# The offsets that order the stages of an attention, FNet and feed-forward kernel, set anew

## The chip, the cores and the metric

The kernel runs on one core of a Trainium2 chip. The metric is the device time of one execution in microseconds (us); several executions are timed and their median is taken. The engines are PE (TensorE, matmuls and transposes), DVE (VectorE), ACT (ScalarE), POOL (GpSimd) and SP (SyncE, which here only issues DMAs); PEld is PE's loading of weights. Each engine works off its own instructions strictly in the order in which they were issued, and an instruction that has to wait holds up all that stand behind it on its engine.

## What is computed

Eight batches of 8 heads, 576 positions and 64 channels each are put through two attentions, whose sum x (8 x 576 x 512) goes through a Fourier mix, a normalization and a feed-forward network:

```python
def _attn_ref(q, k, v):
    ...
    q_d = q.reshape(B, H, Sd, factor, D).mean(axis=3)      # factor 4, Sd = 144
    ...
    out_d = sm_attn(q_d, k_d, v_d)
    out_up = np.repeat(out_d, factor, axis=2)
    mask = np.abs(pos[:, None] - pos[None, :]) < factor
    scores = scale * np.matmul(q, k.transpose(0, 1, 3, 2))
    scores = np.where(mask, scores, -1000000000.0)
    ...
    return (out_up + out_local).astype(np.float32)

def _moe_ref(x, w_ch1, w_ch2):
    X = np.fft.fft(x, axis=1)
    X = np.fft.fft(X, axis=2)
    mixed = np.real(X).astype(np.float32)
    u = x + mixed
    ...
    un = (u - mu) / np.sqrt(var + 1e-06)
    ch = np.maximum(un @ w_ch1, 0.0) @ w_ch2
    return (u + ch).astype(np.float32)
```

## The kernel before

**Pooled attention** (class `Pooled`, one for each batch, called P0 to P7 here). Four copies of v are added up in `vsum`, the first by a DMA from SP, the other three by accumulating DMAs that POOL issues (`sum_v`, L245 to 251). DVE adds up q and k by fours (`sum_in`, L379, five sums for each batch, one for each unit). Then come four steps, each for two heads: scores `sp` on PE (L262), maxima on DVE (L267), exponentials on ACT (L278), transposes `tp` (L288), copies on ACT (L299), the product `avd` with `vsum` (L307) and the division into `odt` (L318 to 322). The result is stored to `ud` in DRAM from SP (L331 to 336).

**Local attention** (class `Unit`, five for each batch, U0.0 to U7.4 here). A unit loads `qkT` (L361, six buffers) and `vaug` (L365, three buffers) from SP; scores `sc` (L386, L393), maxima (L406), exponentials (L411), transposes `tpl` (L423), copies (L443 to 445), products `av` (L452) and the division into `xa` or `xb` (L466 to 470).

**The Fourier mix** (class `Mix`, M0 to M7). Half sums on DVE (L516) and half differences on POOL (L520) of `xa` and `xb` go to `xs` and `xm`; the channels are folded by DVE into `xeo` (L531, L535, also from `odt`), and split into a high and a low part by ACT (`fh`, L542) and POOL (`fl`, L547). The middle channel goes to `z` on ACT and POOL (L556, L557). Four groups of 15 matmuls `y` (L569, called sequence 0 to 3 here) are followed by a copy on ACT (L575) and a difference on DVE (L578); `yz` (L585) does the same for z. Six groups `mix` (L607, three slots, each even and odd) are added on DVE by `mixed` (L611), POOL unfolds them into `oa` and `xm` (L621), and SP stores them to `um` in DRAM in ten DMAs (`store`, L634 and L635).

**The feed-forward part** works on nine blocks of four tiles. Each tile is loaded from `um` by SP (L706), to which POOL accumulates `ud` (L704); DVE and POOL take its statistics (L713 to 717; `rstd` on POOL), DVE normalizes (`un`, L724), PE transposes (`tpn`, L732), ACT and DVE split the result into `unT` (L738, L741). Then come 16 chunks of weights: `hps` (L761) and `acc` (L779 to 781). The first chunks of block 0 and then of block 1 are worked off while the other weights still come in. The weights are decoded once from 64-bit words, in 64 quarters: fetched into `raw` from SP (L146), sized on ACT (L156), clamped on POOL (L161), joined on DVE (L169 to 175), split on ACT and POOL (L186, L190). Most of the quarters come behind the attention.

**What sets the order.** Every step of all these is entered in one list with a time; the times are sums of a stage's start (20 for each batch, 4 for each unit) and an offset from the table `AT` (L22 to 52). The list is sorted by the time (L904 to 906) and issued in that order:

```python
    with tc.manual_schedule():
        for _, _n, fn in sorted(events, key=lambda e: e[:2]):
            fn()
```

So the offsets are no times on the chip: they only set which step stands ahead of which in each engine's row. Waits between engines follow from the tiles that steps share, and from the buffers that they are given in that order. PSUM banks are given out in turn (`bank`): eight in turn before the feed-forward part, four afterwards.

Four times that closes of memory hang on are worked out from the table too (`t_b`, `t_a`, `t_e`, `t_d`): `close_b` (L830) opens the tiles of block 0 in memory that P7 used, `close_a` (L835) the rest of what the first weights need once the last unit is done.

Of the kernel before, what the change touches and what calls it, by code (L numbers as in the profile page):

```python
# [13 lines left out]
ALU = mybir.AluOpType  # L14
# [6 lines left out]
PACE = 20  # L21
AT = {  # L22

    "pooled": (0.6, -0.5, -1.8, -3.1, -3.53),
    "mix": (18.44, 18, 18),

    "local_steps": (0, 1.49, 2.84, 5.24, 5.74, 7.85, 9.25),
    "pooled_steps": (0, 1.58, 2.63, 5.13, 5.73, 7.82, 9.41),

    "qk": (-11.61, 2.5),  # L30
    "sums": (-3.57, 0.79),
    "sum_v": (-10.83, -9.1, -1.92, 1.96),
    "load_v": (3.13,),

    "store_pooled": (1,),
    "pooled_splits": (0.3, 0.9, 0.26, 1.1, 1.34),

    "halves": (0.26, 3.82, 0.35, 3.58),
    "splits": (1.11, 4, 0.49, 1.7, 2.25),
    "z": (0.86, 9.92, 12.49, 12.91, 14.07),  # L40
    "sequence": (13.12, 1.11, 2.15, 3.28),
    "mixed": (19.5, 1.61, 1.13, 2.66, 2.85),

    "ffn": (7.51, 1.51),

    "decode": (49.7, 10.23, 5.84, 1.23, 2.64),
    "decode_steps": (-0.57, 0.24, 0.83, 1.83, 2.17),
    "first_norms": (0.83, 0.7, 2.16, 0.81),
    "second_norms": (-0.5, 0.43, 0.64, 0.83),

    "add": (2.5, 2.04, 2.98),
}


# [11 lines left out]
def kernel(  # L66
# [68 lines left out]
    class Quarter:  # L135


        def __init__(self, n):
            self.f, self.w, self.j = n // 4, 1 + n // 2 % 2, n % 2
            self.n = n  # L140
# [73 lines left out]
    def bank(name, rows=P):  # L214
        banks.append(banks.pop(0))
        return banks[-1].tile([P, DM], F32, name=name, tag="ps")[:rows]
# [21 lines left out]
    sums = {}  # L238
# [253 lines left out]
    halves = [[pf.tile([P, NSL, DM + 2], F32, name=f"x{h}{i}") for h in "sm"] for i in range(2)]  # L492
# [13 lines left out]
    class Mix:  # L506


        def __init__(self, b):
            self.b, self.x, self.y = b, {}, {}  # L510
            self.fh = self.z = None


# [79 lines left out]
        def mix(self, t, odd):  # L593

            n = slots[t][1]
            cols = slice(P * t, P * t + n)
            ps = self.ps = bank("mix", n)
            mms = []
            for T in (2 * odd, 2 * odd + 1):
                mh, ml = chanm[:, 0, T, :], chanm[:, 1, T, :]  # L600
                lh, ll = self.yh[:, T, cols], self.yl[:, T, cols]
                mms += [(lh, mh), (lh, ml), (ll, mh)]
            if not odd:
                mms.append((yz[:, cols], signs.unsqueeze(1).to_broadcast([P, HD, 2])))
            for i, (l, r) in enumerate(mms):
                to = ps if len(r.shape) == 2 else ps.rearrange("p (n two) -> p n two", two=2)
                nc.tensor.matmul(to, l, r, start=(i == 0), stop=(i == len(mms) - 1))  # L607

        def mixed(self, t, odd):
            x = (self.xm if odd else self.xs)[: slots[t][1], t, :DM]  # L610
            nc.vector.scalar_tensor_tensor(  # L611
                out=x, in0=x, scalar=0.5, in1=self.ps, op0=ALU.mult, op1=ALU.add
            )

        def unfold(self, t):
# [21 lines left out]
        def plan(self):  # L637
# [23 lines left out]
            for T in range(4):  # L661
                u = t + first + step * T
                at(u, self.sequence, T)
                at(u + high, self.sequence_high, T)
                at(u + low, self.sequence_low, T)
            first, step, mixed, unfold, store = AT["mixed"]
            for i in range(NSL):
                for odd in range(2):
                    u = t + first + step * (2 * i + odd)
                    at(u, self.mix, i, odd)  # L670
                    at(u + mixed, self.mixed, i, odd)
                at(u + unfold, self.unfold, i)
# [197 lines left out]
    t = t_a + AT["ffn"][0]  # L870
    starts = {}
    for n, f0, f1 in [(0, 0, ROUND), (1, 0, ROUND), (0, ROUND, NF)] + [(n, ROUND * (n == 1), NF) for n in range(1, NBLK)]:
        starts[n] = t
        t = blocks[n].plan(t, f0, f1)
# [15 lines left out]
    t = 0.0  # L890
    for n, x in enumerate(quarters):
        if x.f < CHUNKS[0]:
            decode(n, first + step * n, ahead)
        else:
            begin = [t_a + ahead_later, t_e, t_d][sum(x.f >= c for c in CHUNKS[1:3])]
            t = max(t + step_later, begin + 0.3)
# [139 lines left out]
```

## Time and profile before

| what | us |
|---|---|
| median of 3 executions | 1250.11 |
| lowest and highest of them | 1248.47, 1251.0 |
| the profiled execution, its own time | 1254.06 |
| its span (first to last instruction) | 1252.0 |
| from the first `hps` to the end of the span | 821.32 |

The profiled execution is 3.95 us longer than the median. Its span leaves out 2.06 us of its own time. The span has two parts. Up to 430.68 us the attentions and the mix of eight batches run interleaved: the pooled attention and the units of one batch beside the mixes of the two batches ahead of it. From there on, PE works off the blocks of the feed-forward part with hardly a gap. A stretch of a batch begins, in the rows below, where PE takes up the first `sp` of that batch: batch 1 at 48.60 us, batch 2 at 93.22 us. The granted clock of PE, 1.00 being 2.4 GHz, is a mean over a stretch; 0.50 is the lower level, 1.2 GHz.

### The profile page before, as it was taken

The page shows a single profiled execution, that of the slowest core. Times are in us where ns is not written, and L with a number is a line of the kernel's source. Part 1 is how long each engine was busy: PE and PEld are TensorE (multiplying, and loading weights), DVE is VectorE, ACT ScalarE, POOL GpSimd, SP SyncE. Part 2 cuts the span into 40 slices and gives each one's busy share as a digit, 9 for nine tenths or more (in the row PEclk, how much of TensorE's full clock was granted, in tenths as well). Part 3 has the DMA queues.
Part 4 walks back from the last instruction along what each step waited for, and adds up shares of the span by engine and source line. Part 5 has one row for each costly group of instructions (what it writes and reads, how often), then busy time and mean ns, then how long its engine had stood idle before and what let it go on. Part 6 is the DMA issues. An engine that isn't in the chain of part 4 may idle for free.

```text
span 1252.0 us, 20525 instructions
## 1 busy us (share of the span) xinstructions
PE 1184.1 (95%) x8336; PEld 981.2 (78%) x8336; DVE 590.7 (47%) x1218; ACT 356.0 (28%) x1038; POOL 318.2 (25%) x397
## 2 busy tenths in 40 slices
PE   5889998899995699999999999999999999999998
PEld 5777887787984578888888888888888888888887
DVE  3767778698877788853222222122122222221211
ACT  3655454555562333431111111111011111111100
POOL 2226355365456566531010010000100100100000
PEclk7888998999997799999999999999999999999999
DMA  9755484565645525314040120210400400300000
GB/s 293 197 169 134 128 238 110 162 196 172 163 127 153 133 77 155 119 51 101 5 97 1 52 50 1 78 25 1 99 3 1 101 1 1 101 1 1 34 1 34
DMA packets 50462, 111.45 MB, mean 89 GB/s; under 512 B 6120, under 2 KB 6248, under 8 KB 50040
## 3 DMA queue, kind: packets, MB, share of 16 engines
q1 hardware_dynamic: 42000, 88.66, 22.6%
q0 software_dynamic: 8368, 21.48, 9.3%
q8 instruction: 66, 1.08, 0.4%
q14 instruction: 28, 0.23, 0.1%
HBM read 81.82 MB, written 28.34 MB: 88 GB/s over the span
## 4 chain that ended last, share of the span: by engine, by line
PE 81%; DVE 10%; DMA 6%; POOL 1%; SPq 1%; issue 1%; ACT 1%; POOLq 0%
PE hps L761 31%; PE acc L779 10%; PE acc L781 10%; PE acc L780 10%; PE y L569 4%; PE mix L607 4%; DMA vsum<-in_vg_dram 3%; PE av L452 2%; DMA qkT<-in_qk_dram 2%; PE avd L307 2%; PE sc L393 1%; DVE sums L379 1%; DVE xeo L535 1%; PE tpn L732 1%; PE sp L262 1%
## 5 line engine op out<-in xcount | busy, mean ns | idle before, releaser
L761 PE MATMUL hps<-unT,w1h 128*128 128x512 f32 x1152 | 311.5, 392 | 0.6 <-DVE yl L578 0.6
L769 DVE SCALAR_TENSOR_TENSOR hl<-hps,hh 128x512 fp32r<-128x512 f32 x144 | 99.3, 690 | 437.3 <-ACT hh L765 437.3
L761 PEld LDWEIGHTS hps<-unT,w1h 128*128 128x128 f32 x1152 | 215.2, 188 | 46.7 <-DVE yl L578 0.8
L765 ACT ACTIVATE hh<-hps 128x512 fp32r<-128x512 f32 x144 | 86.2, 598 | 512.1 <-PE hps L761 512.0
L779 PE MATMUL acc<-w2h,hh 128*128 128x512 f32 x576 | 226.5, 393 | 0.0
L781 PE MATMUL acc<-w2h,hl 128*128 128x512 f32 x576 | 225.1, 391 | 0.0
L780 PE MATMUL acc<-w2l,hh 128*128 128x512 f32 x576 | 225.0, 391 | 0.0
L761 PE MATMUL hps<-unT,w1l 128*128 128x512 f32 x576 | 155.2, 391 | 0.0
L761 PEld LDWEIGHTS hps<-unT,w1l 128*128 128x128 f32 x576 | 108.1, 188 | 23.8
L781 PEld LDWEIGHTS acc<-w2h,hl 128*128 128x128 f32 x576 | 108.2, 188 | 23.6
L779 PEld LDWEIGHTS acc<-w2h,hh 128*128 128x128 f32 x576 | 108.1, 188 | 22.9
L780 PEld LDWEIGHTS acc<-w2l,hh 128*128 128x128 f32 x576 | 108.2, 188 | 22.8
L717 POOL TENSOR_TENSOR rstd<-rstd,mhalf 128x1 f32<-128x1 f32 x36 | 20.3, 564 | 341.4 <-DVE rstd L716 341.4
L704 POOL DMA_DIRECT2D ut<-ud x40 | 35.5, 1111 | 208.0 <-DMA ut<-um 207.7
L607 PE MATMUL mix<-chanm,yh 128*128 128x512 f32 (+1 forms) x192 | 65.8, 425 | 5.6 <-DVE xs L611 3.7
L411 ACT ACTIVATE sb<-sc,mx 128x64 f32<-128x64 f32 x320 | 69.8, 329 | 1.3
L741 DVE TENSOR_TENSOR unT<-tpn,unT 128x512 fp32r<-128x512 f32 x36 | 24.8, 690 | 90.4 <-ACT unT L738 90.4
L547 POOL TENSOR_TENSOR fl<-xeo,fh 128x512 fp32r<-128x512 f32 (+1 forms) x40 | 56.0, 1404 | 30.5 <-ACT fh L542 30.2
L379 DVE TENSOR_REDUCE sums<-qkT 128x224 f32<-128x896 f32 (+4 forms) x48 | 44.5, 947 | 27.9 <-DMA qkT<-in_qk_dram 19.6
L520 POOL TENSOR_TENSOR xm<-xa,xb 128x512 f32<-128x512 f32 x24 | 34.2, 1427 | 87.9 <-DVE xb L470 79.9
L738 ACT CAST unT<-tpn 128x512 fp32r<-128x512 f32 x36 | 21.0, 586 | 113.5 <-PE tpn L732 113.5
L452 PE MATMUL av<-vaug,pT 64*64 64x65 f32 x1280 | 48.5, 227 | 1.7 <-DVE odt L322 1.5
(102 smaller groups left out, 1579.7 us busy)
## 6 DMA issues: line engine op xcount, KB each, us to landing
qkT<-in_qk_dram SPq DMA_DIRECT2D x40, 512.0 KB
raw<-in_wq_dram SPq DMA_DIRECT2D x64, 256.0 KB
vaug<-in_vw_dram SPq DMA_DIRECT2D x40, 260.0 KB
ud<-odt SPq DMA_DIRECT2D x16, 576.0 KB
out_dram<-ut SPq DMA_DIRECT2D x36, 256.0 KB
ut<-um SPq DMA_DIRECT2D x32, 256.0 KB
ut<-ud POOLq DMA_DIRECT2D x32, 256.0 KB, 5.6
vsum<-in_vg_dram POOLq DMA_DIRECT2D x24, 292.5 KB, 4.5
```

The costliest lines, as they stand in the source:

```text
L379: nc.vector.tensor_reduce(out=to, in_=x[:, :, a - g0 : e - g0], axis=AX.X, op=ALU.add)
L411: nc.scalar.activation(out=self.sb[:, a], in_=self.sc[:, a * W : (a + 1) * W], func=AF.Exp, scale=0.125, bias=self.mx[:, a : a + 1],)
L452: nc.tensor.matmul(av[r, a, :], pT[r, 4 * hh + a], va[r, 4 * hh + a, :], start=True, stop=True)
L547: nc.gpsimd.tensor_sub(out=l, in0=self.x[t], in1=h.bitcast(F32))
L569: nc.tensor.matmul(y, l, r, start=(i == 0), stop=(i == len(mms) - 1))
L607: nc.tensor.matmul(to, l, r, start=(i == 0), stop=(i == len(mms) - 1))
L761: nc.tensor.matmul(hps, a[:, c, :], unT[:, x, c, :], start=(i == 0), stop=(i == len(mms) - 1))
L765: nc.scalar.activation(out=hh, in_=self.hps[f], func=AF.Relu)
L769: nc.vector.scalar_tensor_tensor(out=hl, in0=self.hps[f], scalar=0.0, in1=self.hh[f].bitcast(F32), op0=ALU.max, op1=ALU.subtract)
L779: nc.tensor.matmul(acc, hh, w2h, start=start, stop=False)
L780: nc.tensor.matmul(acc, hh, w2l, start=False, stop=False)
L781: nc.tensor.matmul(acc, hl, w2h, start=False, stop=stop)
```

## The change

All offsets of `AT` are set anew, each by less than 6 units of its list time. No operation is added, removed or given another shape. Since several `mix` results of one batch may now be open at a time, `Mix.ps` becomes a dictionary with an entry for each slot and half. Two lines of the table stand for the rest:

```diff
-    "sum_v": (-10.83, -9.1, -1.92, 1.96),
+    "sum_v": (-12.68, -6.88, -1.99, 2.95),
...
-    "mixed": (19.5, 1.61, 1.13, 2.66, 2.85),
+    "mixed": (21.24, 1.83, 2.15, 4.71, 7.35),
...
-            self.b, self.x, self.y = b, {}, {}
+            self.b, self.x, self.y, self.ps = b, {}, {}, {}
...
-            ps = self.ps = bank("mix", n)
+            ps = self.ps[t, odd] = bank("mix", n)
...
-                out=x, in0=x, scalar=0.5, in1=self.ps, op0=ALU.mult, op1=ALU.add
+                out=x, in0=x, scalar=0.5, in1=self.ps[t, odd], op0=ALU.mult, op1=ALU.add
```

What this does to the rows of the engines is shown at three places.

**Place A: SP, the loads of batch 4's units.** `um_66` is the DRAM result of M1, `qkT` and `vaug` are inputs of units of batch 4. Before, the last three of the ten stores, behind which a part of the loads stands:

```order
L634 DMA um_66<-xm_136 56x2x512
L634 DMA um_66<-xm_136 2x1x512
L635 DMA um_66<-xm_136 3x512
L361 DMA qkT<-in_qk_dram 128x1024
L365 DMA vaug<-in_vw_dram 128x520
L361 DMA qkT<-in_qk_dram 128x1024
L146 DMA raw<-in_wq_dram 128x512
L361 DMA qkT<-in_qk_dram 128x1024
L365 DMA vaug<-in_vw_dram 128x520 x2
```

After, the loads, behind which the first of the ten stores stands:

```order
L361 DMA qkT<-in_qk_dram 128x1024
L365 DMA vaug<-in_vw_dram 128x520
L361 DMA qkT<-in_qk_dram 128x1024 x2
L365 DMA vaug<-in_vw_dram 128x520
L361 DMA qkT<-in_qk_dram 128x1024
L146 DMA raw<-in_wq_dram 128x512
L365 DMA vaug<-in_vw_dram 128x520
L634 DMA um_66<-oa 56x3x512
```

Before, three of the five `qkT` loads of a batch stand behind the store of the mix; now all five stand ahead of it. The same holds for the other batches that have such a store.

**Place B: POOL, the small `z` of M1** (`xs_135` and `xm_136` are its halves; `oa` and `xm_134` are the unfolding of M0). Before:

```order
L520 TENSOR_TENSOR xm_136<-xa,xb 128x512
L547 TENSOR_TENSOR fl<-xeo,fh 72x512 x2
L251 DMA vsum<-in_vg_dram 72x1040
L557 TENSOR_TENSOR z<-xs_135,z 128x3
L621 TENSOR_TENSOR oa<-xs_133,xm_134 128x512
L621 TENSOR_TENSOR xm_134<-xs_133,xm_134 128x512
```

After:

```order
L520 TENSOR_TENSOR xm_136<-xa,xb 128x512
L547 TENSOR_TENSOR fl<-xeo,fh 128x512
L547 TENSOR_TENSOR fl<-xeo,fh 72x512
L557 TENSOR_TENSOR z<-xs_135,z 128x3
L161 TENSOR_SCALAR wt<-wt 128x256
L251 DMA vsum<-in_vg_dram 72x1040
L621 TENSOR_TENSOR oa<-xs_133,xm_134 128x512
```

The accumulating DMA of `vsum`, which can't be issued before the one ahead of it has landed, stood right ahead of `z`; now it stands behind it.

**Place C: the passage to the feed-forward part, on POOL** (`ut` are the four tiles of block 0, `ud_57` the pooled result of batch 0). Before:

```order
L547 TENSOR_TENSOR fl<-xeo,fh 72x512 x2
L190 TENSOR_TENSOR w2l_87<-wt,w2h_86 128x256
L621 TENSOR_TENSOR oa<-xs_133,xm_134 128x512
L621 TENSOR_TENSOR xm_134<-xs_133,xm_134 128x512
L704 DMA ut_5791<-ud_57 128x512
L704 DMA ut_5792<-ud_57 128x512
L704 DMA ut_5793<-ud_57 128x512
L704 DMA ut_5794<-ud_57 128x512
L547 TENSOR_TENSOR fl<-xeo,fh 128x512
L520 TENSOR_TENSOR xm_136<-xa,xb 128x512
L717 TENSOR_TENSOR rstd<-rstd,mhalf 128x1 x2
L557 TENSOR_TENSOR z<-xs_135,z 128x3
```

After:

```order
L704 DMA ut_5776<-ud_57 128x512
L704 DMA ut_5777<-ud_57 128x512
L704 DMA ut_5778<-ud_57 128x512
L704 DMA ut_5779<-ud_57 128x512
L547 TENSOR_TENSOR fl<-xeo,fh 72x512
L621 TENSOR_TENSOR oa<-xs_133,xm_134 128x512
L621 TENSOR_TENSOR xm_134<-xs_133,xm_134 128x512
L520 TENSOR_TENSOR xm_136<-xa,xb 128x512
L547 TENSOR_TENSOR fl<-xeo,fh 128x512
L557 TENSOR_TENSOR z<-xs_135,z 128x3
L717 TENSOR_TENSOR rstd<-rstd,mhalf 128x1 x2
```

The four loads now stand ahead of two unfoldings and a split that were ahead of them, and six operations stand between them and the first two `rstd`, where two stood.

**The same passage on PE.** `tpn` are the transposes of block 0 (four for each tile), `yz` the matmuls of M7, `mix` the last one of M6. Before:

```order
L607 MATMUL mix<-chanm,yl 64x512
L732 MATMUL tpn<-ident,un 128x128 x8
L585 MATMUL yz<-seqg,z 2x320 x2
L585 MATMUL yz<-seqm,z 2x320 x3
L585 MATMUL yz<-seqg,z 2x320 x2
L585 MATMUL yz<-seqm,z 2x320 x3
L732 MATMUL tpn<-ident,un 128x128 x4
```

After:

```order
L607 MATMUL mix<-chanm,yl 64x512
L585 MATMUL yz<-seqg,z 2x320 x2
L585 MATMUL yz<-seqm,z 2x320 x3
L585 MATMUL yz<-seqg,z 2x320 x2
L585 MATMUL yz<-seqm,z 2x320 x3
L732 MATMUL tpn<-ident,un 128x128 x16
L569 MATMUL y<-seqg,fh 128x320 x2
```

`yz` moved ahead of all `tpn`. Further ahead, two `mix` groups of M6 stood between the last `av` of the kernel and the first `tpn`; now there are four, and sequence 3 and the first two `mix` groups of M6, which stood ahead of the last `avd` (P7's fourth step), stand behind it. On SP the store of M6 moved back past six `raw` fetches.

## Rows read from the trace of the kernel before

**Rows 1.** Windows by stretch: length, busy us (instructions) of PE, PEld, DVE, ACT, POOL; PEclk, DMA share, GB/s

```profile
48.60:93.22 44.62, 40.98 (x556) 35.37 (x556) 29.82 (x75) 25.13 (x89) 14.55 (x17) 0.88 0.54 150
93.22:143.10 49.88, 45.76 (x576) 38.67 (x577) 36.61 (x85) 24.61 (x88) 21.60 (x23) 0.90 0.57 158
189.19:241.87 52.68, 46.91 (x591) 38.89 (x587) 40.13 (x90) 26.95 (x95) 23.94 (x26) 0.94 0.57 154
241.87:288.88 47.01, 44.68 (x587) 37.98 (x587) 40.08 (x93) 26.61 (x95) 24.08 (x26) 0.96 0.62 173
288.88:334.49 45.61, 43.38 (x591) 36.86 (x588) 40.69 (x90) 26.64 (x95) 24.83 (x26) 1.00 0.62 179
391.90:430.68 38.78, 14.71 (x72) 12.04 (x72) 24.68 (x53) 8.64 (x21) 25.80 (x32) 0.65 0.78 193
430.68:1252.00 821.32, 816.54 (x3640) 670.18 (x3638) 270.76 (x497) 137.85 (x272) 114.20 (x164) 1.00 0.17 46
```

**Rows 2.** Timeline before batch 4 (start, length, engine line operation [idle before <-releaser])

```profile
171.29 3.10 SPq L634 DMA_DIRECT2D um<-oa  x4
...
180.51 0.42 SPq L361 DMA_DIRECT2D qkT<-in_qk_dram  x1
...
187.84 1.05 DVE L379 TENSOR_REDUCE sums<-qkT 128x216 f32<-128x864 f32 x1 [0.46 <-DMA qkT<-in_qk_dram]
...
191.43 0.41 PE L288 MATMUL tp<-ident,sd 72*72 72x72 f32 x4 [1.15 <-DVE xb L470]
```

**Rows 3.** Timeline of POOL and PE at the local `z` of batch 1

```profile
117.69 0.84 POOL L251 DMA_DIRECT2D vsum<-in_vg_dram  x1 [3.76 <-DMA vsum<-in_vg_dram]
...
118.80 0.96 PE L585 MATMUL yz<-seqm,z 128*2 128x320 f32 x3 [1.49 <-POOL z L557]
```

**Rows 4.** Window of PE alone: length, busy us (instructions), PEclk, DMA share, GB/s

```profile
115.00:130.00 15.00, 12.58 (x117) 0.66 0.74 177
```

**Rows 5.** The chain that ended last, two of its links on PE

```profile
361.69 2.24 PE y L569 x15
...
379.07 3.02 PE mix L607 x13
```

**Rows 6.** Timeline of the passage to the feed-forward part, all engines

```profile
381.93 1.20 PE L307 MATMUL avd<-vsum,ptd 72*72 72x65 f32 x16
...
390.07 1.39 DVE L172 SCALAR_TENSOR_TENSOR wt<-raw,wt 128x256 int32<-128x256 int32 x1
...
392.03 1.76 SPq L706 DMA_DIRECT2D ut<-um  x4
...
396.82 3.59 POOL L704 DMA_DIRECT2D ut<-ud  x4
...
405.01 0.69 DVE L713 BATCH_NORM_STATS2 st<-ut 128x6 f32<-128x512 f32 x1 [6.99 <-DMA ut<-ud]
...
408.39 1.09 PE L732 MATMUL tpn<-ident,un 128*128 128x128 f32 x4 [16.31 <-DVE un L724]
...
422.44 0.43 ACT L156 ACTIVATE wt<-raw 128x256 f32<-128x256 f32 x1 [7.07 <-DMA raw<-in_wq_dram]
...
424.43 0.90 PE L569 MATMUL y<-seqg,fh 72*128 72x320 f32 x2 [5.40 <-DVE unT L741]
...
430.68 1.10 PE L761 MATMUL hps<-unT,w1h 128*128 128x512 f32 x4
```

**Rows 7.** Groups by line, shapes together: busy us, mean ns | idle before

```profile
L547 POOL TENSOR_TENSOR fl<-xeo,fh 128x512 fp32r<-128x512 f32 (+1 forms) x40 | 56.0, 1404 | 30.5 <-ACT fh L542 30.2
L379 DVE TENSOR_REDUCE sums<-qkT 128x224 f32<-128x896 f32 (+4 forms) x48 | 44.5, 947 | 27.9 <-DMA qkT<-in_qk_dram 19.6
```

**Rows 8.** Groups by line, each shape apart: busy us, mean ns | idle before

```profile
L172 DVE SCALAR_TENSOR_TENSOR wt<-raw,wt 128x256 int32<-128x256 int32 x64 | 43.0, 672 | 2.2
...
L406 DVE TENSOR_REDUCE mx<-sc 128x8 f32<-128x512 f32 x40 | 27.3, 684 | 2.8 <-PE sc L393 2.6
```

**Rows 9.** Timeline of PE: the first scores of batch 1

```profile
48.60 1.24 PE L262 MATMUL sp<-sums 64*72 64x144 f32 x8 [5.36 <-DVE sums L379]
```

More of the change, by code (lines that the diff above doesn't have):

```diff
@@ L22 @@
 AT = {
[L24 to L31, printed above, removed]
-    "sum_v": (-10.83, -9.1, -1.92, 1.96),
[L33 to L41, printed above, removed]
-    "mixed": (19.5, 1.61, 1.13, 2.66, 2.85),
[L44 to L51, printed above, removed]
+    "pooled": (-0.82, -1.16, -2.92, -3.66, -3.97),
+    "mix": (19.33, 19.44, 19.47),
+    "local_steps": (0, 2.01, 2.74, 4.55, 6.44, 7.99, 9.17),
+    "pooled_steps": (0, 1.64, 3.1, 4.52, 5.5, 6.86, 9.7),
+    "qk": (-9.97, 2.23),
+    "sums": (-2.11, 0.4),
+    "sum_v": (-12.68, -6.88, -1.99, 2.95),
+    "load_v": (4.86,),
+    "store_pooled": (1.6,),
+    "pooled_splits": (0.63, 1.63, 0.39, 1.17, 2.21),
+    "halves": (-1.52, 4.16, 1.15, 3.59),
+    "splits": (1.09, 4.71, 0.22, 0.85, 2.73),
+    "z": (1.77, 8.73, 11.56, 12.33, 13.17),
+    "sequence": (15.17, 1.12, 1.12, 2.9),
+    "mixed": (21.24, 1.83, 2.15, 4.71, 7.35),
+    "ffn": (9.61, 1.41),
+    "decode": (49.18, 9.54, 2.02, 1.18, 3.21),
+    "decode_steps": (-0.73, -0.25, 0.7, 1.96, 3.89),
+    "first_norms": (1.46, 0.91, 3.69, 0.74),
+    "second_norms": (-2.92, 1.41, 5.09, 1.68),
+    "add": (1.13, 1.19, 5.36),
 }
```

## The prediction, made before the changed kernel had run

> **What bounds the kernel now.** I read the windows by stretch first, then the timelines at those stretches that are longer than their like, and last the two orders against each other.
>
> From the first `hps` on PE is busy 816.54 of 821.32 us at a granted clock of 1.00 [rows 1]. No operation changes, so this part can't become shorter by more than its 4.8 us of gaps, and I see nothing in the new order that touches it. What can be won lies in the first 430.68 us.
>
> There PE's work is nearly the same for each batch from the third on, so the best stretch shows what a batch needs: 45.61 us, at a clock of 1.00 [rows 1]. The stretch of batch 4 takes 52.68 us, that of batch 5 47.01 us, that of batch 2 49.88 us. In each of these the clock is under 1.00, and PE stands for a part of them. The passage from 391.90 to 430.68 us holds 14.71 us of PE's work in 38.78 us. So PE is the bound, but it loses time in three ways: it waits, it works behind a wait at a lower clock, and at the passage it has nothing to do.
>
> **The passage (place C).** Between the last `avd` of P7 at 381.93 us and the first `hps` at 430.68 us lie 48.75 us [rows 6]. The chain there: SP issues the `um` loads at 392.03 us, POOL the `ud` loads from 396.82 us on, behind two splits, a weight part and two unfoldings; they have landed at 405.01 us, when DVE's statistics begin after 6.99 us of waiting; `tpn` follows at 408.39 us, PE having stood for 16.31 us. Later PE stands 5.40 us ahead of sequence 0 at 424.43 us, because ACT waited 7.07 us for `raw` at 422.44 us, whose fetch stands on SP behind the ten stores of M6 [rows 6].
>
> The new order changes three things. First, sequence 3 and the first two `mix` of M6 stand behind P7's last `avd`: 2.24 us and about 3.02 us [rows 5], 5.3 us of PE's work that now fills a part of the 16.31 us and lies no longer ahead of 381.93 us. Second, M6's store is moved behind six fetches, so the 5.40 us should go. The price is that the six fetches are in front of the store; nobody waits for `um` of M6 until blocks far behind. Third, POOL issues the `ud` loads earlier in its row, but six operations stand then ahead of the first `rstd`, where two stood. Five of these I price at 1.4 us by the mean of L547 [rows 7], the `z` at little: 7 us. If POOL is done with issuing at 400.4 us as before (396.82 + 3.59), it comes to `rstd` at about 407.5 us, beside 406.2 us before, which I take from 405.01 plus the three steps of statistics. So `tpn` comes 1.5 us later against the last `avd`, at 28.0 us behind it instead of 26.5.
>
> From the first `tpn` to the first `hps` it took 22.3 us, and without the 5.40 us it takes 16.9. That makes 28.0 + 16.9 = 44.9 us instead of 48.75, a gain of 3.9 us, and the 5.3 us of work that lie behind 381.93 us now, and ahead of it before, come to it: **-9 us**. Bounds: 0, if the first `tpn` comes later by as much as is won, and -16, if it comes 1.5 us no later and the `ud` loads land earlier by the two splits and two unfoldings that they no longer stand behind (4 by 1.4, 5.6 us). I take 9 because the `um` loads wait for `ud` of P7 to be stored and can't move much against 381.93 us.
>
> **The loads of the next batch (place A).** Before, SP works off the ten stores from 171.29 us on, and can't begin before the mix is unfolded; the last `qkT` load of batch 4 is issued at 180.51 us and its sum begins at 187.84 us, 7.33 us later [rows 2]. PE then waits for what DVE had put off behind the sums: 1.15 us at 191.43 us [rows 2], and more small ones, and works at a lower clock. What it costs is what the stretches have over 45.61 us: 7.07 us for batch 4, 1.40 us for batch 5 [rows 1]. Now all five loads stand ahead of the stores, and need only a free buffer. **-8.5 us**, if both come down to 45.61; bounds -14 (batch 1 and batch 7's part as well, whose stretches begin and end with other work) and 0 (SP's wait goes, but the loads then wait for their buffers).
>
> **`z` ahead of the `vsum` load (place B).** POOL stood 3.76 us with the accumulating load, `yz` on PE stood 1.49 us for `z` behind it [rows 3], and in the 15 us from 115.00 on the granted clock was 0.66 on the mean [rows 4], which is about two thirds of them at 1.2 GHz. The stretch of batch 2 has 4.27 us over 45.61 [rows 1]; I take **-4 us** of it. Bounds -6 and 0. The `vsum` load now waits with fewer instructions behind it that anyone needs soon.
>
> **The start.** In the new order P1's first `sp` stands behind the second `sc` group of batch 0 and the first `av`, which wait for P0's `avd`. The first `sp` of batch 1, now at 48.60 us after a wait of 5.36 us [rows 9], comes then at 50.8 by my laying of the row, with 0.6 us more work done ahead of it: **+2 us**. Bounds 0 and +5, the wait that is there now.
>
> **New short covers.** In the steady part nothing is turned around, but some steps follow each other more closely. Sequence 2 takes the bank of a unit's result, and the `tp` of the first pooled step comes right behind sequence 3. About one sequence group, 2.24 us [rows 5], covers what DVE or ACT have to do meanwhile, which needs about as much. Where such a cover was missing, PE waited 1.15 us [rows 2]. Seven batches by 0 to 1.15 us are 0 to 8 us; I take 0.4 us each, since cover and need are nearly equal: **+3 us**.
>
> **The sum.** -9 - 8.5 - 4 + 2 + 3 = -16.5 us on the profiled execution's 1254.06 us, so 1237.6 us. The median of the runs lies 3.95 us below that execution: 1233.6, so 1234 us. A measurement of this kernel tells changes of about 0.2%, 2.5 us, from none.
>
> **Rival A: POOL becomes the bound of the passage.** The six operations ahead of `rstd` meet DVE's joins, halves and foldings. In the passage of before, a join beside two splits of POOL took 1.39 us at 390.07 us [rows 6], and 0.672 us on the mean of all 64 [rows 8]: 0.7 us lost on one instruction. Nine such meetings on the chain to `tpn` are 6.5 us, with the later issue of the loads that follows 9 us, which is all that the passage wins. Then it is -7.5 us in all, 1246.6 us for the execution and 1242.6 us for the median. For it speaks that POOL is busy 25.80 of 38.78 us there already [rows 1]; against it, that half of these operations lie between the loads' issue and their landing, when DVE has nothing to do. The Trainium skill has a rule for this ("SBUF — State Buffer", section "Who interferes with whom"): an instruction of DVE with two inputs from SBUF and one of GpSimd that reads SBUF hold a shared port pair in turn, each for its whole length. By that rule each meeting costs as much as the POOL operation has left, so the collisions would be nearer to rival A's than to mine; the 1.39 us agree with it.
>
> **Rival B: the sums of a batch come late; slower.** The five sums of a batch, 44.5/8 = 5.6 us [rows 7], now stand in one row on DVE between the results of a batch's second and third unit, with a local maxima of 0.68 us [rows 8] and two results, for which I take three times as much, 2.0 us: 8.3 us. A unit's share of a stretch is 45.61/5 = 9.1 us. Likewise the last `qkT` load can't begin before the fourth unit's scores leave their buffer, and needs 7.33 + 1.05 = 8.4 us [rows 2] where the next batch's `sp` comes a unit's share later, 9.1 us. So both have a margin of 0.7 to 0.8 us. If a load takes over 8.1 us, or DVE is behind by over 0.8 us, PE waits at the third unit's bank or at `sp`, the clock falls, and the stretch is as long as batch 4's was: 7.07 us lost. With three of the six stretches so, it is -16.5 + 21 = +4.5 us: 1258.6 us, 1254.6 us for the median. For it speaks how thin the margin is, and a DMA share of 0.62 in a good stretch [rows 1]; against it, that a load waits for no store any more, and that all margins are above zero.
>
> **Rival C: the waits only move.** PE waits less at one place and as much at the next: the passage gives 4, the loads give 4, the start takes 5, the covers 3: 0 us, 1254 us and 1250 us for the median.
>
> **Chances.** Forecast 0.62 (its own range 1222 to 1242 us), rival A 0.17, rival B 0.13, rival C 0.08. The range goes from 1217 us, which the bounds of the passage and the loads together would go past only by a little, to 1253 us: it takes in A and C, and leaves out most of B and the lower tail. Faster by over 0.2%: the forecast and A nearly whole, 0.79. Within it: C and an edge of A, 0.07. Slower: B and the upper edge of C, 0.14.
>
> **What would show it.** In the changed kernel's windows the stretches of batches 4 and 5 should be near 45.6 us at a clock of 1.00, that of batch 2 near 46. The wait of `yz` for `z` should be gone. From P7's last `avd` to the first `hps` it should be 45 us, with a wait ahead of the first `tpn` of about 12 us and none over 1 us ahead of sequence 0. Batch 1's `sp` should come at 50 to 51 us. The first `hps` should come at about 414 us. I am wrong if PE waits for `sums` or for the bank of sequence 2 in each batch, or if `tpn` comes over 30 us behind that `avd`.

## The result, and the profile after

The changed kernel takes 1232.12 us in the median (1227.79 to 1232.71), the kernel before in the same comparison 1250.55 us: a ratio of 0.9843 (95% interval 0.9812 to 0.9874). Run once more beside later kernels it took 1230.67 us, 0.9829 (0.9803 to 0.9856). The forecast was 1234 us, and faster.

The profiled execution of the changed kernel took 1231.77 us (span 1229.7 us), 22.3 us less than that of before. Where they went is read from windows of PE between the same four places in both kernels: the first `sp` of batch 1, the first `sp` of batch 7, the last `avd`, the first `hps`. First the kernel before, PE alone (length, busy us (instructions), PEclk, DMA share, GB/s); its last stretch stands in [rows 1]:

```profile
48.60:334.49 285.89, 265.61 (x3479) 0.94 0.59 164
334.49:381.93 47.44, 47.30 (x616) 1.00 0.34 97
381.93:430.68 48.75, 24.68 (x182) 0.72 0.70 178
```

The same view of the changed kernel, which has the last stretch too:

```profile
50.79:307.47 256.68, 248.64 (x3450) 0.99 0.63 183
307.47:360.60 53.13, 48.85 (x611) 0.94 0.34 95
360.60:409.01 48.41, 31.26 (x211) 0.75 0.65 166
409.01:1229.70 820.69, 816.29 (x3640) 1.00 0.17 46
```

| from, to | before | after | difference |
|---|---|---|---|
| start to first `sp` of batch 1 | 48.60 | 50.79 | +2.2 |
| to first `sp` of batch 7 | 285.89 | 256.68 | -29.2 |
| to the last `avd` | 47.44 | 53.13 | +5.7 |
| to the first `hps` | 48.75 | 48.41 | -0.3 |
| to the end | 821.32 | 820.69 | -0.6 |

The counts in brackets say what work was moved across the borders. Batches 1 to 6 hold 29 matmuls fewer, the passage 29 more. At 2.24/15 = 0.15 us each [rows 5] that is 4.4 us, the forecast's 5.3 us to within a microsecond. So, between these two executions, batches 1 to 6 won about 25 us, and the passage about 5, since it does more in the same time. Batch 7 up to its last `avd` lost 6 to 7 us. The feed-forward part is as it was.

A part of the passage's 5 us is chance. Five further executions below keep one of the two orders there: with that of before it took 45.53 and 46.27 us (the first two experiments), with the new one 48.64, 46.75 and 48.46 us (the changed kernel again, and the two edits of it that lie elsewhere and move `vsum` and a join). By the means, 46.9 us before and 48.1 after, the passage with its 4.4 us of added work won about 3 us.

The 25 us of batches 1 to 6 are of two kinds. PE's idle time, length minus busy, fell from 20.3 to 8.0 us: 25 waits of 0.2 to 1.9 us, at 18 kinds of steps, became nine of 0.2 to 2.1 us. The rest, some 12 us, is work that no longer ran at the lower clock: 0.94 on the mean before, 0.99 after. Three stretches of the changed kernel, which answer to the rows of batches 2, 4 and 5 in [rows 1]:

```profile
87.96:130.12 42.16, 40.47 (x569) 1.00 0.58 172
...
174.84:218.60 43.76, 42.85 (x592) 1.00 0.66 190
218.60:262.22 43.62, 43.29 (x591) 1.00 0.64 188
```

Batch 5 has 0.3 us of idle time in 43.6, at a clock of 1.00: by PE's idle time another order of the same operations could win no more than that there.

The passage in the changed kernel, first PE (start, length, instruction [idle before <-releaser]):

```profile
386.80 0.96 PE L585 MATMUL yz<-seqm,z 128*2 128x320 f32 x3 [10.46 <-POOL z L557]
...
389.92 1.11 PE L732 MATMUL tpn<-ident,un 128*128 128x128 f32 x4 [0.82 <-DVE un L724]
393.36 1.09 PE L732 MATMUL tpn<-ident,un 128*128 128x128 f32 x4 [2.33 <-DVE un L724]
...
399.11 1.12 PE L732 MATMUL tpn<-ident,un 128*128 128x128 f32 x4 [3.32 <-DVE un L724]
...
409.01 1.09 PE L761 MATMUL hps<-unT,w1h 128*128 128x512 f32 x4
```

These answer to [rows 6]. The wait of 16.31 us is now one of 10.46, ahead of `yz`; the wait ahead of sequence 0 is gone. New are 6 us of waits between the four tiles, since joins of weights (L169 to L175) stand ahead of the second and the fourth `un` on DVE:

```profile
391.39 0.29 DVE L169 TENSOR_SCALAR wt<-wt 128x256 int32<-128x256 int32 x1
...
392.52 0.69 DVE L724 TENSOR_SCALAR un<-ut,mv,rstd 128x512 f32<-128x512 f32 x1
...
394.54 0.48 DVE L169 TENSOR_SCALAR wt<-wt 128x256 int32<-128x256 int32 x1
...
395.51 1.37 DVE L175 SCALAR_TENSOR_TENSOR wt<-raw,wt 128x256 int32<-128x256 int32 x1
...
397.41 1.64 DVE L724 TENSOR_SCALAR un<-ut,mv,rstd 128x512 f32<-128x512 f32 x1
```

The last `un` also takes 1.64 us, beside an unfolding on POOL; where POOL stands still it takes 0.54. Before, a join stood ahead of the third `un` (412.57 to 414.92 us), but there PE had `yz` to work on and waited only 0.52 us. That the joins are the cause is read from these rows; no run took them away. DVE and POOL at the first statistics:

```profile
382.58 0.69 DVE L713 BATCH_NORM_STATS2 st<-ut 128x6 f32<-128x512 f32 x1 [6.46 <-DMA ut<-ud]
383.52 0.15 DVE L716 TENSOR_SCALAR rstd<-mv 128x1 f32<-128x1 f32 x1
```

```profile
380.51 1.91 POOL L621 TENSOR_TENSOR oa<-xs,xm 128x512 f32<-128x512 f32 x1
382.50 1.26 POOL L621 TENSOR_TENSOR xm<-xs,xm 128x512 f32<-128x512 f32 x1
383.72 1.47 POOL L520 TENSOR_TENSOR xm<-xa,xb 128x512 f32<-128x512 f32 x1
385.16 1.25 POOL L547 TENSOR_TENSOR fl<-xeo,fh 128x512 fp32r<-128x512 f32 x1
386.38 0.37 POOL L557 TENSOR_TENSOR z<-xs,z 128x3 fp32r<-128x3 f32 x1
386.72 0.57 POOL L717 TENSOR_TENSOR rstd<-rstd,mhalf 128x1 f32<-128x1 f32 x1
```

The first statistics are done on DVE at 383.67 us, but POOL comes to the first `rstd` at 386.72, 3 us later, working without a gap.

Batch 7 has one wait that the kernel before does not have there. DVE, POOL and PE:

```profile
326.29 2.73 DVE L172 SCALAR_TENSOR_TENSOR wt<-raw,wt 128x256 int32<-128x256 int32 x1
329.06 1.37 DVE L175 SCALAR_TENSOR_TENSOR wt<-raw,wt 128x256 int32<-128x256 int32 x1
330.35 1.48 DVE L535 TENSOR_TENSOR xeo<-xm 128x256 f32<-128x256 f32 x1
...
332.14 0.42 DVE L322 TENSOR_TENSOR odt<-avd,rsd 72x256 f32<-72x256 f32 x1
```

```profile
326.24 1.28 POOL L547 TENSOR_TENSOR fl<-xeo,fh 72x512 fp32r<-72x512 f32 x1 [1.41 <-ACT fh L542]
327.48 1.26 POOL L621 TENSOR_TENSOR oa<-xs,xm 128x512 f32<-128x512 f32 x1
328.82 1.33 POOL L621 TENSOR_TENSOR xm<-xs,xm 128x512 f32<-128x512 f32 x1
330.11 1.44 POOL L520 TENSOR_TENSOR xm<-xa,xb 128x512 f32<-128x512 f32 x1
```

```profile
332.62 0.73 PE L607 MATMUL mix<-chanm,yh 128*128 128x512 f32 x2 [3.58 <-DVE odt L322]
```

L172, L175 and L535, which take 0.42 us where POOL stands still, end 0.28 us after an operation of POOL each time: 329.02 after 328.74, 330.43 after 330.15, 331.83 after 331.55. Three instructions lose 4.3 us, the pooled result behind them is late, and PE stands 3.58 us for the bank that it frees. This is the rule that the prediction cited for its rival A (the Trainium skill, "SBUF — State Buffer", section "Who interferes with whom"): the trace agrees, with whole operations of POOL waited out and not a share of them.

### The profile page after: what moved, and what is told of

The parts are those of the page before. It is cut to its first block, busy times and chain, and to the rows that moved or that the text cites. A ratio compares the mean times of both kernels' runs of the same rounds, so it can differ in the third digit from the quotient of the medians.

```text
span 1229.7 us, 20578 instructions
## 1 busy us (share of the span) xinstructions
PE 1173.7 (95%) x8336; PEld 977.8 (80%) x8336; DVE 595.5 (48%) x1218; ACT 355.8 (29%) x1038; POOL 312.1 (25%) x397
## 4 chain that ended last, share of the span: by engine, by line
PE 80%; DVE 10%; DMA 5%; issue 2%; ACT 1%; POOL 1%; SPq 1%; DVEq 0%; POOLq 0%
PE hps L761 32%; PE acc L779 11%; PE acc L781 11%; PE acc L780 11%; PE y L569 4%; PE mix L607 3%; DMA vsum<-in_vg_dram 2%; PE av L452 2%; PE sc L393 2%; PE avd L307 1%; PE tpn L732 1%; DMA qkT<-in_qk_dram 1%; DVE wt L172 1%; DVE sums L379 1%; DVE xeo L535 1%
## 5 line engine op out<-in xcount | busy, mean ns | idle before, releaser
L547 POOL TENSOR_TENSOR fl<-xeo,fh 128x512 fp32r<-128x512 f32 (+1 forms) x40 | 53.2, 1335 | 35.4 <-ACT fh L542 35.4
L452 PEld LDWEIGHTS av<-vaug,pT 64*64 64x64 f32 x1280 | 43.3, 141 | 9.4 <-issue 3.6
L393 PEld LDWEIGHTS sc<-qkT 64*64 64x64 f32 x1280 | 46.6, 141 | 3.4 <-issue 0.8
```

The source lines that it names most:

```text
L393: nc.tensor.matmul(sc[r, a * W : (a + 1) * W], self.qkT[r, 0, a // 2, o : o + W], self.qkT[r, 1, a // 2, o : o + W], start=False, stop=Tru ...
L452: nc.tensor.matmul(av[r, a, :], pT[r, 4 * hh + a], va[r, 4 * hh + a, :], start=True, stop=True)
L547: nc.gpsimd.tensor_sub(out=l, in0=self.x[t], in1=h.bitcast(F32))
```

## The experiments

Each ratio is to the kernel before, run on the same chip. A stretch of batch b goes from its first `sp` to the next batch's.

**One part of the change alone: the stores of the mix late.** In the kernel before:

```diff
-            at(u + store, self.store)
+            at(u + (store if self.b >= B - 2 else 11.65), self.store)
```

> The kernel before, with one thing of the change: the stores of M0 to M5 stand on SP behind the five qkT loads that three of them stood ahead of; all other engines keep their order. The changed kernel's stretches of batches 2 to 6 are 4 to 9 us shorter than before. Theory A (the late loads were the cause in batches 3 to 6): the stretch of batch 4 goes from 52.68 to under 46 us, that of batch 5 from 47.01 to under 46, batch 3 by 1 to 2 us; 8 to 13 us less in all, ratio 0.990 to 0.993. Rival (the loads were late, but something on DVE or PE stood at the same places, and the new offsets of the other steps gave the gain): batch 4 stays over 50 us, ratio 0.998 or more. Batch 2's stretch stays near 49.9 us by both.

Measured: 1246.11 us, ratio 0.9959 (0.9935 to 0.9983). What DVE waited for ahead of the sums, and the stretches of batches 4 and 5, PE alone:

```profile
L379 DVE TENSOR_REDUCE sums<-qkT 128x224 f32<-128x896 f32 (+4 forms) x48 | 44.0, 944 | 16.1 <-PE sp L262 8.5 <-DMA qkT<-in_qk_dram 7.4
```

```profile
190.53:238.00 47.47, 43.86 (x591) 1.00 0.60 165
238.00:282.80 44.80, 43.37 (x591) 1.00 0.65 182
```

DVE stood 7.4 us for `qkT` instead of 19.6 [rows 7], and PE's waits for `sums` and `xb` in batches 4 to 6, four with 4.0 us before, are gone: the mechanism is as theory A has it. Batch 4 is shorter by 5.2 us of its 52.68, batch 5 by 2.2 of its 47.01, but this is not all place A's: in the next experiment, where the stores stand early as before, batch 4 took 47.23 us too. The size is read from the medians: 5 us, about half of what was expected; batch 4 kept four other waits, 3.6 us together.

**Another part alone: `z` ahead of the `vsum` load.** In the kernel before:

```diff
-    "sum_v": (-10.83, -9.1, -1.92, 1.96),
+    "sum_v": (-10.83, -8.5, -1.92, 1.96),
```

> The kernel before, with one thing of the change: the local z of each mix stands on POOL ahead of the vsum load that stood ahead of it; nothing else moves. Theory B (the stalled POOL queue made batch 2's loss): the wait of 1.49 us of yz is gone, the granted clock from 115 to 130 us is near 1.00 instead of 0.66, batch 2's stretch goes from 49.88 to about 45.5 us; 3 to 5 us less, ratio 0.996 to 0.998. Rival: yz waits for something else at the same place, batch 2 stays over 49 us, ratio 0.999 or more.

Measured: 1253.5 us, ratio 1.0014 (0.9996 to 1.0032): nothing won. The wait of `yz` is gone, and batch 2 is shorter, but batch 3 is longer by as much. Batches 2 and 3:

```profile
93.26:140.54 47.28, 44.63 (x577) 0.93 0.61 166
140.54:189.03 48.49, 45.24 (x589) 0.97 0.60 163
```

Batch 2 took 49.88 us before [rows 1], batch 3 46.09 us at a clock of 1.00. In this execution 2.4 of the 2.6 us won were lost again one batch later, one in waits and the rest at a lower clock; why the clock fell there now and not before stays open. Further on batch 4 took 47.23 us and batch 6 49.15, beside 52.68 and 45.61 before: single batches differ by several us from one execution to the next, so that nothing was won is said by the medians.

**The stores early again in the changed kernel.**

```diff
-                at(pooled_at(self.b) + first + step * self.m, fn)
+                at(pooled_at(self.b) + (-1.35 + 0.005 * self.m if fn == self.load and self.b > 2 and self.m > 1 else first + step * self.m), fn)
...
-            at(u + store, self.store)
+            at(u + (store if self.b >= B - 2 else 4.76), self.store)
```

> The changed kernel (profiled execution 1231.77 us) with place A undone: on SP the stores of M0 to M5 stand ahead of the last three qkT loads of the next batch again; the order of the other engines is that of the changed kernel. Theory A: the stretches of batches 3 to 6, 43.6 to 45.3 us in the changed kernel, grow by 2 to 8 us each, 9 to 20 us in all, about 1241 to 1252 us. Rival (with the new order of the other steps the loads have time enough even behind the store): under 3 us more, about 1233 us.

Measured: 1284.45 us, ratio 1.0253 (1.0231 to 1.0276), 52 us over the changed kernel; no theory had so much. Only SP's order was altered. SP, DVE and PE ahead of batch 4:

```profile
176.97 2.77 SPq L634 DMA_DIRECT2D um<-oa  x4
...
183.13 1.34 SPq L361 DMA_DIRECT2D qkT<-in_qk_dram  x3
```

```profile
187.90 2.40 DVE L379 TENSOR_REDUCE sums<-qkT 128x96 f32<-128x384 f32 x3 [9.08 <-DMA qkT<-in_qk_dram]
```

```profile
191.70 1.24 PE L262 MATMUL sp<-sums 64*72 64x144 f32 x8 [8.02 <-ACT wt L156]
```

The store waits for the last unfolding, which comes later in the new order; SP stood from 159.18 to 176.97 us, the loads behind it came at 183, DVE stood 9.08 us for them, PE 8.02 (the profile names ACT; the sums ended at 191.55 us, just ahead). PE waits like this, for 7 to 9 us, at the first `sp` of five batches. So the store's place is worth 5 us in the old order and 52 in the new: the new order has later unfoldings, and can have them only because the loads no longer stand behind the store.

**The `vsum` load ahead of `z` again in the changed kernel.**

```diff
-    "sum_v": (-12.68, -6.88, -1.99, 2.95),
+    "sum_v": (-12.68, -8.3, -1.99, 2.95),
```

> The changed kernel with place B undone: the second accumulating vsum load stands on POOL ahead of the local z, of a split and of a clamp again; nothing else moves. Theory B: yz waits for z by 1 us or more in some batches, and the clock falls behind it: 3 to 6 us more, about 1235 to 1238 us. Rival (SP issues the first vsum load earlier in the new order, so POOL has nothing to wait for): POOL's wait ahead of the load is under 1 us, and the time stays at 1232 us.

Measured: 1227.68 us, ratio 0.9808 (0.9785 to 0.9831), no slower than the changed kernel. POOL came to the moved load without a wait in batches 2 to 7, and no `yz` waited for `z`. The rival holds: place B brings nothing that can be measured, in either order.

**The changed kernel again**, as the measure for the next three.

> The changed kernel once more, unaltered, beside the next three on the same chip: their differences of some us are read against it. All theories: 1228 to 1233 us, and the same waits as in its first profile: 10.5 us of PE ahead of yz in the passage, 3.6 us ahead of a mix in batch 7.

Measured: 1230.67 us. The first `sp` of batch 1 came at 49.84 us here, at 50.79 in the first execution, and between 46.68 and 50.98 us in the others that have the changed kernel's order up to there. With the order of before it came at 48.60, 50.25 and 48.99 us. So the start differs by more from one execution to the next than the forecast's term for it.

**The unfoldings of M6 out of the passage.**

```diff
-                at(u + unfold, self.unfold, i)
+                at(t + 40.5 + i if self.b == B - 2 else u + unfold, self.unfold, i)
-            at(u + store, self.store)
+            at(t + 42.6 if self.b == B - 2 else u + store, self.store)
```

> The changed kernel with the three unfoldings of M6 on POOL, and its store on SP, moved behind the statistics of block 0: four operations of 1.3 to 2.2 us leave POOL's row there, two of them ahead of the first rstd. In the changed kernel the first statistics are done at 383.67 us and the first rstd begins at 386.72 us, POOL working without a gap in between. Theory (POOL's row sets the first tpn, the sixth of the prediction's operations): yz and the first tpn come 2.5 to 3 us earlier against the last avd, 2.5 to 4 us less in all, about 1228 us. Rival (the landing of ud or DVE's own row sets it): POOL idles there instead, under 1 us less.

Measured: 1235.09 us, ratio 0.987 (0.9843 to 0.9897), 4 us slower than the changed kernel. In the passage the theory held, with less than it said: the first `tpn` came 27.7 us behind the last `avd`, beside 29.6 in the changed kernel again, so 1.9 us earlier and not 2.5 to 3, and the first `hps` at 403.97 us, beside 408.35. But from there to the end it took 827.8 us instead of 820.7. DVE and PE behind the first `hps`:

```profile
411.52 1.37 DVE L169 TENSOR_SCALAR wt<-wt 128x256 int32<-128x256 int32 x1 [0.71 <-POOL wt L161]
412.92 1.46 DVE L172 SCALAR_TENSOR_TENSOR wt<-raw,wt 128x256 int32<-128x256 int32 x1
```

```profile
425.23 1.11 PE L732 MATMUL tpn<-ident,un 128*128 128x128 f32 x4 [4.65 <-DVE un L724]
```

The unfoldings now stand among the clamps of the weights: DVE's joins wait for these and collide with those, and `un` of block 1 stands behind the joins.

**A join of weights moved off the pooled result of batch 7.**

```diff
-            at(t + d, fn)
+            at(t + d + (0.75 if n == 10 and fn == x.join else 0), fn)
```

> The changed kernel with the join of one weight quarter (number 10, three DVE instructions) moved behind the first pooled result of batch 7 and a local maxima on DVE. In the changed kernel these three and one folding took 2.73, 1.37 and 1.48 us there beside POOL's row, and PE stood 3.58 us for the result behind them, with the clock at 0.67 for the next ten us. Theory (the collided join holds up the result, and this is the 6.6 us that batch 7 loses): the wait ahead of that mix falls under 1 us, batch 7's stretch up to the last avd from 53.1 to about 48 us; 4 to 6 us less, about 1226 us. Rival (the result is late by its own matmuls, or the next step collides with POOL in the same way): under 1.5 us less.

Measured: 1224.97 us, ratio 0.9783 (0.9757 to 0.9809), 5.7 us less than the changed kernel beside it. This is the lowest median of all kernels here. Batch 7 up to the last `avd`, PE alone, and the pooled result on DVE:

```profile
306.10:354.11 48.01, 45.87 (x610) 1.00 0.39 104
```

```profile
325.37 0.42 DVE L322 TENSOR_TENSOR odt<-avd,rsd 72x256 f32<-72x256 f32 x1
...
327.62 1.46 DVE L172 SCALAR_TENSOR_TENSOR wt<-raw,wt 128x256 int32<-128x256 int32 x1
```

48.01 us instead of 53.13, at a clock of 1.00 instead of 0.94. The join still collides (1.46 us instead of 0.42), only nothing that PE waits for stands behind it.

**Both.** The two edits together.

> Both edits of the two kernels above in the changed kernel. If both theories hold, their gains add up, since they lie in different stretches: 6.5 to 10 us less than the changed kernel, about 1223 us. Rival (what is won in batch 7 is given back in the passage, where PE waits for the block's first tile anyway): no more than the better of the two alone.

Measured: 1228.93 us, ratio 0.982 (0.9796 to 0.9843): slower than the join's move alone. The gains don't add up, because one of them is none: first `hps` at 400.50 us, then 827.0 us to the end, as with the unfoldings moved alone.

**The old attention offsets in the changed kernel** (`pooled`, `local_steps`, `pooled_steps`, `qk`, `sums`, `sum_v`, `load_v`, `store_pooled` as before).

```diff
-    "pooled": (-0.82, -1.16, -2.92, -3.66, -3.97),
+    "pooled": (0.6, -0.5, -1.8, -3.1, -3.53),
...
-    "local_steps": (0, 2.01, 2.74, 4.55, 6.44, 7.99, 9.17),
+    "local_steps": (0, 1.49, 2.84, 5.24, 5.74, 7.85, 9.25),
```

> The changed kernel with the offsets of the attention steps (pooled and local steps, loads, sums, stores) as before; the offsets of the mix and of the feed-forward part stay new. From the first sp of batch 1 to that of batch 7 PE stood 20.2 us in 25 waits before and 7.7 us in 9 waits in the changed kernel. Theory W (the gain there lies in the whole set, whose halves lean on each other, as the store of the mix does on the loads): more waits than before's 20 us, over 1250 us. Rival (additive: each half brings its part): between the two kernels, 1236 to 1245 us, with 10 to 17 us of waits.

Measured: 1264.02 us, ratio 1.0104 (1.0082 to 1.0125). PE stood 25.6 us in batches 1 to 6, 14.7 of them, in three waits of up to 6.7 us of a `tp`, for `xs` (L611), the step that frees the mix's banks.

**The old mix offsets in the changed kernel** (`mix`, `pooled_splits`, `halves`, `splits`, `z`, `sequence`, `mixed` as before).

```diff
-    "sequence": (15.17, 1.12, 1.12, 2.9),
-    "mixed": (21.24, 1.83, 2.15, 4.71, 7.35),
+    "sequence": (13.12, 1.11, 2.15, 3.28),
+    "mixed": (19.5, 1.61, 1.13, 2.66, 2.85),
```

> The changed kernel with the offsets of the mix (halves, splits, z, sequences, mixes, unfoldings, store) as before; the attention's and the feed-forward part's stay new. The store of a mix then stands ahead of three or four loads again. Theory W: over 1250 us, with PE standing more than the 20.2 us of before in batches 1 to 6. Rival (additive): 1236 to 1245 us.

Measured: 1285.05 us, ratio 1.0272 (1.0247 to 1.0297). PE stood 38.8 us in batches 1 to 6, 21.3 of them for `vaug` loads, which stand behind the store on SP. One of them:

```profile
342.97 2.00 PE L452 MATMUL av<-vaug,pT 64*64 64x65 f32 x32 [7.29 <-DMA vaug<-in_vw_dram]
```

Both halves are slower than either whole: theory W.

**The old offsets of the feed-forward part in the changed kernel** (`ffn`, `decode`, `decode_steps`, `first_norms`, `second_norms`, `add` as before).

```diff
-    "decode": (49.18, 9.54, 2.02, 1.18, 3.21),
-    "decode_steps": (-0.73, -0.25, 0.7, 1.96, 3.89),
+    "decode": (49.7, 10.23, 5.84, 1.23, 2.64),
+    "decode_steps": (-0.57, 0.24, 0.83, 1.83, 2.17),
```

> The changed kernel with the offsets of the feed-forward part (weights' decoding, norms, loads of blocks 0 and 1) as before; attention and mix stay new. Batches 1 to 6 should stay as in the changed kernel, 7 to 8 us of waits, but for the few decoding steps in them. Theory (the passage's gain is the work of M6 moved behind the last avd, which these offsets don't set): passage from the last avd to the first hps within 3 us of the changed kernel's 48.4, total 1230 to 1237 us. Rival (the passage's gain is in the order of loads, rstd and fetches): the passage is 5 us or more longer, over 1238 us.

Measured: 1242.56 us, ratio 0.9926 (0.9906 to 0.9946), 10 to 12 us over the changed kernel. The passage is not longer: from the last `avd` at 370.95 us to the first `hps` at 413.22 it takes 42.3 us, with two sequence groups less in it (4.5 us), which stand behind the first `hps` here. So its gain is not in these offsets. What they bring lies in the batches: batches 1 to 6 took 269.4 us instead of 256.7. PE waits in four batches as the changed kernel does in batch 7 alone:

```profile
201.87 0.74 PE L607 MATMUL mix<-chanm,yh 128*128 128x512 f32 x2 [2.76 <-DVE odt L322]
...
246.88 0.73 PE L607 MATMUL mix<-chanm,yh 128*128 128x512 f32 x2 [2.23 <-DVE odt L322]
295.50 0.79 PE L607 MATMUL mix<-chanm,yh 128*128 128x512 f32 x2 [2.76 <-DVE odt L322]
...
342.97 0.73 PE L607 MATMUL mix<-chanm,yh 128*128 128x512 f32 x2 [2.59 <-DVE odt L322]
```

**The join moved, and two unfoldings moved a little.**

```diff
-                at(u + unfold, self.unfold, i)
+                at(t + 33.28 + i / 4 if self.b == B - 2 and i < 2 else u + unfold, self.unfold, i)
...
-            at(t + d, fn)
+            at(t + d + (0.75 if n == 10 and fn == x.join else 0), fn)
```

> The changed kernel with the join moved as in e6, and the first two unfoldings of M6 moved only as far as behind block 0's rstd and a split, ahead of block 1's loads; M6's store stays. In e5 the late unfoldings brought the first hps 4 to 5 us earlier, and gave 7 us back behind it, where block 1's tpn waited 4.65 us. Theory (both are right, and the give-back is the unfoldings' meeting with block 1's statistics): first hps as early as in e7, about 401 us, no wait of block 1's tpn, 1221 to 1223 us, 2 to 3 us less than e6. Rival (what is won ahead of the first hps is always given back at block 1, whose tiles come no earlier): 1225 us, as e6.

Measured: 1225.88 us, ratio 0.9786 (0.9765 to 0.9807), as with the join alone. The first tile's `tpn` came 1.7 us earlier, at 382.14, the last one no earlier, at 393.94 us beside 393.04, after 4.99 us of waiting for `un`: four unfoldings stand in a row on POOL from 386.04 us on, and beside them a join's three instructions, which stand ahead of the last `un`, took 1.35 to 1.37 us each, and that `un` 1.50 us. The rival's outcome, within the passage already.

## Why the prediction was right

The total was right: -16.5 us forecast on the profiled execution, -22.3 measured on it, -18.4 between the medians, 1234 and 1232.12 us. (The profiled execution of before was a long one, 3.5 us over the median of its comparison, and 2 to 3 of these lie in its passage.) The terms were not right: the steady batches won some 15 us more than forecast, the passage 4 to 6 less, and batch 7 lost 6 to 7 that were not forecast. That their sum came so close is in good part luck.

**The steady batches, -9.5 forecast (-8.5 for place A, -4 for place B, +3 for new covers), about -25 measured.** Place A was the right mechanism: moved alone it brings 5 us. Place B alone brings nothing, in either order; the 4 us were read from a window that held a wait and a low clock, and in the execution with `z` alone moved both came back one batch later. The term for new short covers had its kind right: a sequence waited once, 1.42 us, for a unit's result, and five waits, 5.4 us, stand at steps that did not wait before and that the term does not name. What was put at nothing is the other side. I weighed the few steps that had moved closer to what they wait for, and not the many that had moved away: of the 25 waits of before, 20.2 us, nearly all are gone (those of `tpl` for `rs`, of sequence 0 for `ptd`, of `mix` for `yl`, of `sp` for `sums`, of `yz` for `z` among them), and with them nearly all of the low clock. Which moved step ended which of them is not shown one by one, except for place A; the kernels with half of the old offsets show only that neither the attention's nor the mix's alone do it. The other fault is the floor: I took the best stretch of before, 45.61 us, for what a batch needs, though PE is busy for 43.38 of it at a clock of 1.00 [rows 1]. Batch 5 now takes 43.62 us. With that floor the stretches of batches 2, 4, 5 and 6 would have had 6.5, 9.3, 3.6 and 2.2 us to give, 22 us together.

**The passage, -9 forecast, -5 measured between the profiled executions, about -3 by the means.** The 5.3 us of moved work came, as 4.4, and the 5.40 us wait went. But as a price 5.40 us was too much: in the first two experiments, whose passage has the order of before, this wait was 1.98 and 2.16 us, and the passage itself shorter:

```profile
376.94:422.47 45.53, 26.29 (x183) 0.70 0.75 189
380.77:427.04 46.27, 26.37 (x183) 0.70 0.75 186
```

The step that failed is the 16.9 us from the first `tpn` to the first `hps`: it took 19.1, by DVE's rows because joins part the four `un`. The 16.9 us even held 2.9 us of `yz`, which the new order puts ahead of the first `tpn`. Without them 14.0 us were left, so 5.1 came to it: 3.5 us of waits, 5.9 instead of 2.3, and 1.6 us by which the same matmuls took longer, at a mean clock of 0.60 instead of 0.71. The first `tpn` came 29.3 us behind the last `avd`, 28.0 forecast: POOL's six operations held up the first `rstd` by 3.0 us, 1.3 forecast. That is a part of rival A.

**Batch 7, nothing forecast, +6 to 7 measured.** The collision of DVE with POOL, which rival A sets in the passage, decides here. I had read DVE's row at the sums of the next batch, and not in a batch without them, where unfoldings, splits and a join meet. Nor was the price of 0.7 us a meeting enough: it was taken against a mean, 0.672 us [rows 8], that holds met instructions itself. Against 0.42 us alone the L172 here lost 2.3. That the collision costs this much is shown by moving the join: -5.7 us.

**The start, +2 forecast, +2.2 measured**, of which nothing is shown: with the new order it came at 46.7 to 51.0 us in other executions, with the old one at 48.6 to 50.3.

**Rival B** did not come: no `sp` from batch 2 on waits for `sums` in the changed kernel. The margins of 0.7 us on DVE and on the loads were enough. The experiment with the early stores shows the other side: where they are gone, PE stands 7 to 9 us at the `sp` of five batches.

## What to carry to other kernels

A kernel whose order is written out by hand can lose its time in many waits of about a microsecond, and in the lower clock behind them; count the whole idle time and the clock against the busy time at full clock, not against the best stretch. Such an order is one thing: the better one with the old attention or the old mix in it was slower than all of the old one, so a single moved step says little of what the set will bring. A wait read from one execution is not yet a price: 5.40 us in one were 2 us in two others. Where a stage is longer than its like, look for a collided instruction on DVE and for what stands behind it: moving that instruction behind the step that PE waits for won 5.7 us here.

## What was not expected of the hardware

A DVE instruction that met a row of POOL operations was held for two of them in a row: L172 took 2.73 us at 326.29 us in the changed kernel, 0.42 us where POOL stands still; the three instructions of one weight quarter then took 4.4 us. In the same trace DVE instructions with one of their two inputs in PSUM were not held: L470 (`av`) took at most 0.43 us and L611 (`mix`) at most 0.69, in the 47 and 29 cases beside an operation of POOL as in those without. And ten small stores that wait at the head of SP's queue held up three loads so far that each of five stretches grew by 9 to 12 us.
